# A layernorm, gated-MLP and attention kernel: front loads in one queue in order of need, and transposes placed a tile ahead of use

## The chip, the core and the metric

The kernel runs on one core of a Trainium2 chip. The metric is device time in microseconds (us); one execution is one number. "Before" and "changed" are the two kernels compared; the variants are named e1 to e13. Engines are named as in the profile: PE is TensorE's matmul, PEld its weight load, DVE is VectorE, ACT is ScalarE, POOL is GpSimd, SP is SyncE, which here only issues DMAs.

## The reference, cut to what matters

```python
def reference(A_x, A_k_cache, A_v_cache, A_wq, A_wo, B_x, B_W_gate, B_W_up, B_W_down):
    x = A_x                                    # 1 x 2048 x 512, bf16
    xn = _layernorm(x, axis=-1)
    s = _A_ref(xn, A_k_cache, A_v_cache, A_wq, A_wo)    # 32-head attention over cached K and V
    g = _silu(_B_ref(xn, B_W_gate, B_W_up, B_W_down))   # h = relu(xn Wg) * (xn Wu); h Wd; 512 -> 1792 -> 512
    return x + s * g
```

The gated MLP is computed first, from about 1 to 140 us, and attention fills the rest. The change touches only the first 20 us of code: the loads of `x` and of the gate and up weights, and the first quarter of the gate and up matmuls.

## The kernel before: the parts that matter

Rows of `x` are worked on in four row blocks of 512; a row block has four row tiles of 128. A weight has 14 column blocks (`FC`) of 128. For the first row block the kernel does not wait for the whole layernorm: it centres each row tile, transposes it on PE, and starts the first three column blocks tile by tile (128-column matmuls, "the head"). From column block 3 on it uses full-size matmuls of 512 columns.

The loads come from two queues, SP's and ACT's. Each weight is cut into three column pieces, at blocks 0, 3, 8 and 14:

```python
FCS = [0, min(3, FC), min(8, FC), FC]
HFC = 3
# load_w(engine, tile, source, semaphores, piece); load_x0(engine, row tile); load_xq(row block), on SP
load_x0(sp, 0)
load_x0(act, 1)
load_w(sp, Wg_sb, wg_src, sem_wg, 0)
load_w(act, Wu_sb, wu_src, sem_wu, 0)
load_x0(sp, 2)
load_x0(act, 3)
load_w(sp, Wg_sb, wg_src, sem_wg, 1)
load_w(sp, Wu_sb, wu_src, sem_wu, 1)
load_xq(1)
load_w(sp, Wg_sb, wg_src, sem_wg, 2)
load_w(sp, Wu_sb, wu_src, sem_wu, 2)
for Q in range(2, QB):
    load_xq(Q)
sem_wd.sig(sp.dma_start(Wd_sb[:], ...))
```

The head, with a warm-up of ten and two throw-away matmuls:

```python
warm_mm(10)                       # called just before head_ln
def head_ln():
    ctok = {0: head_transpose(0, head_center(0))}
    warm_mm(2)
    for n in range(4):
        if n + 1 < 4:
            ntok = head_center(n + 1)
        _wait(pe, ctok[n])
        head_tile(n, 0)
        if n + 1 < 4:
            ctok[n + 1] = head_transpose(n + 1, ntok)
        for fc in range(1, HFC):
            head_tile(n, fc)
```

The matmul results go to a ring of three slots, each with a gate bank and an up bank in PSUM. ACT applies the Relu, DVE multiplies, and the product frees the slot. In the same DVE stream, after the product of column block `fc`, come the layernorm statistics of row tile `4 + fc`, because those rows are needed next. DVE takes its instructions in the order of the program, so a product stands behind the statistics that were issued before it, and those wait for the rows to land.

```python
def finish_gate_up(Q, fc, s, gtok, gu_tok):
    # ... ACT: gr = relu(gate bank); DVE: hT = gr * up bank, signalled as h_tok
    ring_tok[s] = [rtok, h_tok]      # the next user of slot s waits for both
    if Q == 0:
        ln_task(fc)

def ln_task(i):
    if i < 4 * (QB - 1):
        ln_hold["st"] = ln_stats(4 + i)      # waits for load_xq((4 + i) // 4) where (4 + i) % 4 == 0
        # ... every fourth: aggregate, and Sqrt on ACT; from i = 4 on, coefficients and normalization on POOL
    # ...
```

The softmax here doesn't subtract the row's maximum and nothing guards it: scores larger than these inputs give would overflow.

Of the kernel before, what the change touches and what calls it, by code (L numbers as in the profile page):

```python
# [51 lines left out]
def bass_recurrent_scan__mha_block_cached__glu_gated_reglu__prompt_kernel(  # L52
# [18 lines left out]
    NQ = 512  # L71
# [33 lines left out]
    with ExitStack() as es:  # L105
# [27 lines left out]
        PT = [S_([128, 2, NQ], BF16, "PT") for _ in range(NPB)]  # L133
        warm = S_([128, D], BF16, "warm")
        es_b = ExitStack()
# [23 lines left out]
        sem_x0 = [newsem(16) for _ in range(4)]  # L159
        sem_wg = [newsem(16) for _ in range(3)]  # L160
        sem_wu = [newsem(16) for _ in range(3)]
        sem_xq = [newsem(16) for _ in range(QB)]
# [39 lines left out]
        with nc.Block() as block:  # L202

            @block.tensor
            def _(_pe_eng):
# [12 lines left out]

                FCS = [0, min(3, FC), min(8, FC), FC]
                HFC = 3  # L220
# [17 lines left out]

                warm_w = sem_ln1.sig(dve.memset(warm[:], 0.0))
                load_x0(sp, 0)  # L240
                load_x0(act, 1)
                load_w(sp, Wg_sb, wg_src, sem_wg, 0)
                load_w(act, Wu_sb, wu_src, sem_wu, 0)
                load_x0(sp, 2)
                load_x0(act, 3)
                load_w(sp, Wg_sb, wg_src, sem_wg, 1)
                load_w(sp, Wu_sb, wu_src, sem_wu, 1)
                if QB > 1:
                    load_xq(1)
                load_w(sp, Wg_sb, wg_src, sem_wg, 2)  # L250
                load_w(sp, Wu_sb, wu_src, sem_wu, 2)
                for Q in range(2, QB):
# [103 lines left out]
                def head_transpose(n, ntok):  # L356
# [13 lines left out]
                    return acc_free[n % 2]  # L370

                def warm_mm(k):
                    for _i in range(k):
                        pe.matmul(ps_r[:, 2 * NSLOT - 1, 0:D], warm[:, 0:128], warm[:], start=True, stop=True)  # L374

                def head_ln():
                    ctok = {0: head_transpose(0, head_center(0))}
                    warm_mm(2)
                    for n in range(4):
                        if n + 1 < 4:  # L380
                            ntok = head_center(n + 1)
                        _wait(pe, ctok[n])
                        head_tile(n, 0)
                        if n + 1 < 4:
                            ctok[n + 1] = head_transpose(n + 1, ntok)
                        for fc in range(1, HFC):
                            head_tile(n, fc)

                half_slots = []

                def head_tile(n, fc):
# [5 lines left out]
                    for i, (W, sems) in enumerate(((Wg_sb, sem_wg), (Wu_sb, sem_wu))):  # L397
                        if n == 0 and fc == 0:
                            pe.wait_ge(sems[0].h, 16)
                        ins = None  # L400
                        for c in range(DC):
                            ins = pe.matmul(ps_r[:, 2 * s + i, hs], W[:, c, fs], xcT[:, c, hs],  # L402
                                            start=(c == 0), stop=(c == DC - 1))
                        if n == 3:
                            half_tok[(fc, i)] = (sem_gate if i == 0 else sem_gu).sig(ins)
# [40 lines left out]
                hT_free = [None, None]  # L446

                def finish_gate_up(Q, fc, s, gtok, gu_tok):
                    par = Q % 2
                    gb = 2 * s  # L450
                    gk = fc % NSLOT
                    _wait(act, gtok)
                    _wait(act, gr_free[gk])
                    rtok = sem_relu.sig(act.activation(gr_sb[gk][:], ps_r[:, gb, :], ACTF.Relu))  # L454
                    _wait(dve, gu_tok)
                    _wait(dve, rtok)
                    if fc == 0:
                        _wait(dve, hT_free[par])
                    h_tok = sem_h.sig(
                        dve.tensor_tensor(hT[par][:, fc, :], gr_sb[gk][:], ps_r[:, gb + 1, :], ALU.mult)  # L460
                    )
                    gr_free[gk] = h_tok
                    ring_tok[s] = [rtok, h_tok]
                    if Q == 0:
                        ln_task(fc)
                    return h_tok

                def emit_gate_up(Q):
                    qs = slice(Q * NQ, (Q + 1) * NQ)
                    h_tok = None  # L470
                    for fc in range(FC):
                        fs = slice(fc * 128, (fc + 1) * 128)
                        if Q == 0 and fc < HFC:
                            s = half_slots[fc]
                            finish_gate_up(Q, fc, s, half_tok[(fc, 0)], half_tok[(fc, 1)])
                            continue
                        s = ring_acquire()
                        gb = 2 * s
                        if fc == 0:
# [7 lines left out]
                        for c in range(DC):  # L487
                            ins = pe.matmul(ps_r[:, gb, :], Wg_sb[:, c, fs], xT[:, c, xs],  # L488
                                            start=(c == 0), stop=(c == DC - 1))
                        gtok = sem_gate.sig(ins)  # L490
                        for c in range(DC):
                            ins = pe.matmul(ps_r[:, gb + 1, :], Wu_sb[:, c, fs], xT[:, c, xs],  # L492
                                            start=(c == 0), stop=(c == DC - 1))
# [44 lines left out]
                assert DC == 4 and QB >= 2 and FC >= 4 * (QB - 1) + 2  # L538
                _wait(pe, warm_w)
                warm_mm(10)  # L540
                head_ln()
# [354 lines left out]
```

## Time and profile before

| | |
|---|---|
| median of three runs | 1286.97 us (1286.95 to 1287.77) |
| span of the profiled execution | 1284.6 us (its time: 1286.42 us) |
| PE busy, of the span | 1278.8 us |
| chain of waits that ended last | 99% PE |
| first full-size gate matmul starts | 12.83 us |
| statistics of row tile 8 (row 1024) start | 19.46 us |

The first view is the busy time of each engine in chosen stretches. The columns are the stretch, its length, busy time and number of instructions of PE, PEld, DVE, ACT and POOL, granted clock, DMA share and GB/s.

```profile
1.19:6.21 5.02, 4.78 (x16) 1.76 (x16) 2.37 (x6) 2.07 (x3) 0.50 (x4) 1.00 0.87 273
6.21:12.83 6.62, 6.20 (x108) 6.06 (x109) 3.15 (x8) 3.25 (x6) 0.00 (x0) 1.00 1.07 363
12.83:140.00 127.17, 127.17 (x590) 57.62 (x591) 56.47 (x104) 40.40 (x71) 12.29 (x16) 1.00 0.32 70
140.00:1275.00 1135.00, 1135.00 (x11300) 767.25 (x11299) 310.85 (x551) 955.31 (x1029) 0.00 (x0) 1.00 0.28 51
```

PE is busy 127.17 of 127.17 us, then 1135.00 of 1135.00. After 12.83 us it has no idle time for an earlier load to remove. A change of the front can only win what lies before 12.83.

The second view is the timeline of before: start, duration, engine, line, operation, `output<-inputs`, shapes, count, and in brackets the idle time before the row and what ended it. It is shown up to the start of the first full-size group.

```profile
1.19 4.12 PE L374 MATMUL ps_r<-warm 128*128 128x512 bf16 x10 [1.19 <-DVE warm L239]
...
6.21 0.40 PE L402 MATMUL ps_r<-xcT,Wg_sb 128*128 128x128 bf16 x4 [0.25 <-ACT xcT L369]
...
12.03 0.39 PE L402 MATMUL ps_r<-xcT,Wu_sb 128*128 128x128 bf16 x4
12.83 1.02 PE L488 MATMUL ps_r<-xcT,Wg_sb 128*128 128x512 bf16 x4 [0.42 <-ACT gr_sb L454]
```

```profile
18.23 0.69 DVE L460 TENSOR_TENSOR hT<-gr_sb,ps_r 128x512 bf16<-128x512 bf16 x1 [0.92 <-PE ps_r L492]
19.46 0.69 DVE L319 BATCH_NORM_STATS2 stats<-x_sb 128x6 f32<-128x512 bf16 x1 [0.54 <-DMA x_sb<-in_A_x_dram]
...
20.35 0.69 DVE L460 TENSOR_TENSOR hT<-gr_sb,ps_r 128x512 bf16<-128x512 bf16 x1
```

```profile
20.60 1.03 PE L492 MATMUL ps_r<-xcT,Wu_sb 128*128 128x512 bf16 x4
21.46 1.03 PE L488 MATMUL ps_r<-xcT,Wg_sb 128*128 128x512 bf16 x4
22.33 1.03 PE L492 MATMUL ps_r<-xcT,Wu_sb 128*128 128x512 bf16 x4
```

PE lost 0.58 us before 12.83: the group of four before it started at 12.03, and four 128-column matmuls take 0.2226 us, so the next could have come at 12.25. At 19.46 DVE had waited 0.54 us for rows 1024 and up. The product behind these statistics ended at 20.35 + 0.69 = 21.04, and the matmuls that need its ring slot started at 21.46. So the load of these rows cost PE nothing, **with 0.42 us to spare**.

### The profile page before, as it was taken

To read this page: it belongs to the slowest core of one execution; us is meant where nothing else is said; L and a number is where in the kernel's file an instruction comes from. 1 tells how busy PE (TensorE), PEld (TensorE's weight loads), DVE (VectorE), ACT (ScalarE), POOL (GpSimd) and SP (SyncE) were. 2 spreads that over 40 slices of the span, in tenths; PEclk is the share of its full clock that TensorE was granted. 3 is DMA by queue.
4 is the path that set the end of the run, shared out by engine and by line. 5 is a ranking of instruction groups with operands and counts; after the bars stand their busy time and mean duration, and the time that the engine had idled before them with its cause. 6 is when DMAs were issued, how large, how long until landed. Compare 5 with 4: busy or idle time off the path is not lost.

```text
span 1284.6 us, 26946 instructions
## 1 busy us (share of the span) xinstructions
PE 1278.8 (100%) x12040; PEld 835.2 (65%) x12040; DVE 380.6 (30%) x685; ACT 1001.7 (78%) x1109; POOL 13.2 (1%) x25
## 2 busy tenths in 40 slices
PE   9999999999999999999999999999999999999998
PEld 5444476666666666666666666666666666666665
DVE  6433311112222222222222222222222222234455
ACT  3322399998888888888888888888888888888884
POOL 2100000000000000000000000000000000000000
PEclk9999999999999999999999999999999999999999
DMA  9600123232222332332321322323323312333202
GB/s 262 131 1 1 22 48 53 62 55 38 36 53 46 71 55 50 55 70 51 54 47 31 66 47 53 55 67 55 55 51 71 54 34 38 51 67 55 51 13 75
DMA packets 240977, 72.13 MB, mean 56 GB/s; under 512 B 227808, under 2 KB 240864, under 8 KB 240864
## 3 DMA queue, kind: packets, MB, share of 16 engines
q1 hardware_dynamic: 240048, 69.76, 28.5%
q8 instruction: 96, 1.57, 0.5%
q10 hardware_dynamic: 816, 0.66, 0.2%
q14 instruction: 17, 0.14, 0.0%
HBM read 32.77 MB, written 2.10 MB: 27 GB/s over the span
## 4 chain that ended last, share of the span: by engine, by line
PE 99%; DVE 1%; ACT 0%; issue 0%; DVEq 0%
PE ps_acc L742 36%; PE ps_r L645 34%; PE ps_r L578 9%; PE ps_r L599 8%; PE ps_acc L511 4%; PE ps_r L488 4%; PE ps_r L492 4%; PE ps_r L779 1%; DVE fin_tmp L787 0%; PE ps_r L402 0%; PE ps_r L374 0%; DVE x_sb L803 0%; ACT gr_sb L454 0%; PE ps_acc L364 0%; ACT xcT L369 0%
## 5 line engine op out<-in xcount | busy, mean ns | idle before, releaser
L655 ACT ACTIVATE PT<-ps_r 128x1024 bf16<-128x1024 f32 x1024 | 952.5, 1054 | 167.7 <-PE ps_r L645 167.7
L742 PEld LDWEIGHTS ps_acc<-V_sb,PT 128*128 128x128 bf16 x8192 | 620.9, 98 | 241.8 <-ACT PT L655 3.5
L742 PE MATMUL ps_acc<-V_sb,PT 128*128 128x129 bf16 x8192 | 776.9, 220 | 0.0
L645 PE MATMUL ps_r<-QT_sb,KT_sb 128*128 128x512 bf16 x2048 | 754.5, 379 | 0.0
L672 DVE RECIPROCAL rz_sb<-ps_acc 128x4 f32<-128x4 f32 x127 | 23.2, 183 | 729.8 <-PE ps_acc L742 729.8
L645 PEld LDWEIGHTS ps_r<-QT_sb,KT_sb 128*128 128x128 bf16 x2048 | 194.9, 98 | 1.1 <-DVE QT_sb L589 0.4
L578 PE MATMUL ps_r<-xnT,Wq_sb 128*128 128x512 bf16 x512 | 130.9, 379 | 0.0
L599 PE MATMUL ps_r<-Wo_sb,OT_store 128*128 128x512 bf16 x448 | 114.6, 379 | 0.0
L589 DVE CAST QT_sb<-ps_r 128x512 bf16<-128x512 f32 x128 | 88.5, 691 | 48.2 <-PE ps_r L578 48.2
L578 PEld LDWEIGHTS ps_r<-xnT,Wq_sb 128*128 128x128 bf16 x512 | 49.8, 97 | 60.7 <-ACT PT L655 27.1
L675 DVE TENSOR_TENSOR Onorm<-ps_acc,rz_sb 128x512 bf16<-128x512 f32 x127 | 87.8, 691 | 4.4
L599 PEld LDWEIGHTS ps_r<-Wo_sb,OT_store 128*128 128x128 bf16 x448 | 43.8, 98 | 52.9 <-ACT PT L655 0.2
L454 ACT ACTIVATE gr_sb<-ps_r 128x512 bf16<-128x512 f32 x56 | 32.9, 595 | 49.2 <-PE ps_r L488 48.7
L612 DVE TENSOR_TENSOR s_acc<-s_acc,ps_r 128x512 f32<-128x512 f32 x96 | 66.0, 687 | 17.4 <-PE ps_r L599 17.4
L460 DVE TENSOR_TENSOR hT<-gr_sb,ps_r 128x512 bf16<-128x512 bf16 x56 | 38.4, 685 | 46.9 <-PE ps_r L492 42.2
L511 PE MATMUL ps_acc<-Wd_sb,hT 128*128 128x512 bf16 x224 | 49.0, 379 | 0.0
L492 PE MATMUL ps_r<-xnT,Wu_sb 128*128 128x512 bf16 x168 | 43.1, 379 | 0.0
L488 PE MATMUL ps_r<-xnT,Wg_sb 128*128 128x512 bf16 x168 | 43.1, 379 | 0.0
L511 PEld LDWEIGHTS ps_acc<-Wd_sb,hT 128*128 128x128 bf16 x224 | 21.9, 98 | 26.5 <-DVE g_sb L528 0.3
L519 ACT ACTIVATE sig_sb<-ps_acc 128x512 f32<-128x512 f32 x12 | 7.2, 597 | 29.5 <-PE ps_acc L511 29.5
L492 PEld LDWEIGHTS ps_r<-xnT,Wu_sb 128*128 128x128 bf16 x168 | 16.4, 98 | 19.8
L488 PEld LDWEIGHTS ps_r<-xnT,Wg_sb 128*128 128x128 bf16 x168 | 16.4, 98 | 19.8
(50 smaller groups left out, 182.1 us busy)
## 6 DMA issues: line engine op xcount, KB each, us to landing
V_sb<-in_A_v_cache_dram SPq DMA_DIRECT2D x32, 512.0 KB, 4.6
Wq_sb<-in_A_wq_dram SPq DMA_DIRECT2D x32, 128.0 KB, 2.5
Wo_sb<-in_A_wo_dram SPq DMA_DIRECT2D x8, 512.0 KB, 4.9
OT_store<-Onorm SPq DMA_TRANSPOSE x127, 2.4
Wd_sb<-in_B_W_down_dram SPq DMA_DIRECT2D x1, 1792.0 KB, 14.6
x_sb<-in_A_x_dram SPq DMA_DIRECT2D x3, 512.0 KB, 12.1
out_dram<-x_sb SPq DMA_DIRECT2D x6, 256.0 KB, 2.2
Wg_sb<-in_B_W_gate_dram SPq DMA_DIRECT2D x1, 768.0 KB, 12.0
```

The lines of the kernel that those rows point to most:

```text
L460: dve.tensor_tensor(hT[par][:, fc, :], gr_sb[gk][:], ps_r[:, gb + 1, :], ALU.mult)
L488: ins = pe.matmul(ps_r[:, gb, :], Wg_sb[:, c, fs], xT[:, c, xs], start=(c == 0), stop=(c == DC - 1))
L492: ins = pe.matmul(ps_r[:, gb + 1, :], Wu_sb[:, c, fs], xT[:, c, xs], start=(c == 0), stop=(c == DC - 1))
L511: ins = pe.matmul(ps_acc[:, jb, 0:D], hT[par][:, fc, j * 128:(j + 1) * 128], Wd_sb[:, fc, :], start=(fc == 0), stop=(fc == FC - 1))
L578: ins = pe.matmul(ps_r[:, bank, :], Wq_sb[b][:, c, :], xnT[:, c, qs], start=(c == 0), stop=(c == DC - 1))
L589: etok = sem_qpe.sig(dve.tensor_copy(QT_sb[b][:, qs], ps_r[:, bank, :]))
L599: ins = pe.matmul(ps_r[:, bank, 0:D], OT_store[g % 2][:, hh, n * 128:(n + 1) * 128], Wo_sb[g % 2][:, hh, :], start=(hh == 0), stop=(hh == ...
L612: dve.tensor_tensor(s_acc[:, n, :], s_acc[:, n, :], ps_r[:, bank, 0:D], ALU.add)
L645: ins = pe.matmul(ps_r[:, 2 * s + tt, :], KT_sb[h % 2][:, t * 128:(t + 1) * 128], QT_sb[h % 2][:, qs], start=True, stop=True)
L655: act.activation(PT[pb][:], ps_r[:, 2 * s:2 * s + 2, :], ACTF.Exp, scale=scale)
L675: dve.tensor_tensor(Onorm[ob][:], o_ap, rz_sb[:].to_broadcast([128, 4, Dh]), ALU.mult))
L742: ins = pe.matmul(o_ap, PT[pb][:, tt, j * 128:(j + 1) * 128], V_sb[vb][:, t, 0:VW], start=(t == 0 and j % 2 == 0), stop=(t == KT - 1 and j ...
```

## The change

Its intent is fourfold: put all early loads but one into one queue, in the order in which they are needed, and cut the first need down to two column blocks of both weights; place each transpose a tile ahead of its use, so that PE does not wait for the copy out of PSUM; put column block 3 into the two accumulator banks, which are free by then, so that it needs no ring slot; and take the warm-up operand from a constant, which saves a memset, with fewer warm-up matmuls.

```diff
-                FCS = [0, min(3, FC), min(8, FC), FC]
+                FCS = [0, 2, 4, 6, 10, FC]
@@ loads (load_wgu(k) loads piece k of both weights, on SP)
-                warm_w = sem_ln1.sig(dve.memset(warm[:], 0.0))
                 load_x0(sp, 0)
                 load_x0(act, 1)
-                load_w(sp, Wg_sb, wg_src, sem_wg, 0)
-                load_w(act, Wu_sb, wu_src, sem_wu, 0)
+                load_wgu(0)
                 load_x0(sp, 2)
-                load_x0(act, 3)
-                load_w(sp, Wg_sb, wg_src, sem_wg, 1)
-                load_w(sp, Wu_sb, wu_src, sem_wu, 1)
-                if QB > 1:
-                    load_xq(1)
-                load_w(sp, Wg_sb, wg_src, sem_wg, 2)
-                load_w(sp, Wu_sb, wu_src, sem_wu, 2)
+                load_x0(sp, 3)
+                load_wgu(1)
+                load_wgu(2)
+                load_xq(1)
+                load_wgu(3)
+                load_wgu(4)
                 for Q in range(2, QB):
                     load_xq(Q)
@@ head
+                    c0 = head_transpose(0, head_center(0))
+                    warm_mm(1)
+                    c1 = head_transpose(1, head_center(1))
+                    n2 = head_center(2)
+                    n3 = head_center(3)
+                    _wait(pe, c0)
+                    head_tile(0, 0)
+                    head_tile(0, 1)
+                    _wait(pe, c1)
+                    head_tile(1, 0)
+                    head_tile(1, 1)
+                    c2 = head_transpose(2, n2)
+                    head_tile(0, 2)
+                    head_tile(1, 2)
+                    c3 = head_transpose(3, n3)
... (tiles 2 and 3 follow; the old loop is gone)
@@ gate and up
-                        s = ring_acquire()
-                        gb = 2 * s
+                        if Q == 0 and fc == HFC:
+                            s = None                    # the two accumulator banks
+                            _wait_all(pe, acc_free)
+                        else:
+                            s = ring_acquire()
+                        g_ps, u_ps = gu_banks(s)
@@ warm-up
-                warm_mm(10)
+                warm_mm(8)
... (weight waits per piece, five semaphores per weight, constants of 1.0 as warm-up operands)
```

More of the change, by code (lines that the diff above doesn't have):

```diff
@@ L133, in bass_recurrent_scan__mha_block_cached__glu_gated_reglu__prompt_kernel @@
         PT = [S_([128, 2, NQ], BF16, "PT") for _ in range(NPB)]
-        warm = S_([128, D], BF16, "warm")
         es_b = ExitStack()
@@ L159, in bass_recurrent_scan__mha_block_cached__glu_gated_reglu__prompt_kernel @@
         sem_x0 = [newsem(16) for _ in range(4)]
-        sem_wg = [newsem(16) for _ in range(3)]
-        sem_wu = [newsem(16) for _ in range(3)]
+        sem_wg = [newsem(16) for _ in range(5)]
+        sem_wu = [newsem(16) for _ in range(5)]
         sem_xq = [newsem(16) for _ in range(QB)]
@@ L237, in load_xq, with load_wgu @@
                         sp.dma_start(x_sb[:, 4 * Q:4 * Q + 4, :], x_t[:, 4 * Q:4 * Q + 4, :]))
-                warm_w = sem_ln1.sig(dve.memset(warm[:], 0.0))
+                def load_wgu(k):
+                    load_w(sp, Wg_sb, wg_src, sem_wg, k)
+                    load_w(sp, Wu_sb, wu_src, sem_wu, k)
                 load_x0(sp, 0)
                 load_x0(act, 1)
-                load_w(sp, Wg_sb, wg_src, sem_wg, 0)
-                load_w(act, Wu_sb, wu_src, sem_wu, 0)
+                load_wgu(0)
                 load_x0(sp, 2)
-                load_x0(act, 3)
-                load_w(sp, Wg_sb, wg_src, sem_wg, 1)
-                load_w(sp, Wu_sb, wu_src, sem_wu, 1)
-                if QB > 1:
-                    load_xq(1)
-                load_w(sp, Wg_sb, wg_src, sem_wg, 2)
-                load_w(sp, Wu_sb, wu_src, sem_wu, 2)
+                load_x0(sp, 3)
[4 more added lines that the diff above has]
+                load_wgu(4)
                 for Q in range(2, QB):
@@ L370, in head_transpose @@
                     return acc_free[n % 2]
+                ones_w = nc.const_aps.tensor(1.0, [128, 128], BF16)
+                ones_r = nc.const_aps.tensor(1.0, [128, NQ], BF16)
                 def warm_mm(k):
                     for _i in range(k):
-                        pe.matmul(ps_r[:, 2 * NSLOT - 1, 0:D], warm[:, 0:128], warm[:], start=True, stop=True)
+                        pe.matmul(ps_r[:, 2 * NSLOT - 1, :], ones_w, ones_r, start=True, stop=True)
                 def head_ln():
-                    ctok = {0: head_transpose(0, head_center(0))}
-                    warm_mm(2)
-                    for n in range(4):
-                        if n + 1 < 4:
-                            ntok = head_center(n + 1)
-                        _wait(pe, ctok[n])
-                        head_tile(n, 0)
-                        if n + 1 < 4:
-                            ctok[n + 1] = head_transpose(n + 1, ntok)
-                        for fc in range(1, HFC):
-                            head_tile(n, fc)
+                    c0 = head_transpose(0, head_center(0))
[13 more added lines that the diff above has]
+                    c3 = head_transpose(3, n3)
+                    _wait(pe, c2)
+                    for fc in range(HFC):
+                        head_tile(2, fc)
+                    _wait(pe, c3)
+                    for fc in range(HFC):
+                        head_tile(3, fc)
                 half_slots = []
@@ L397, in head_tile @@
                     for i, (W, sems) in enumerate(((Wg_sb, sem_wg), (Wu_sb, sem_wu))):
-                        if n == 0 and fc == 0:
-                            pe.wait_ge(sems[0].h, 16)
+                        if n == 0 and fc in FCS:
+                            pe.wait_ge(sems[FCS.index(fc)].h, 16)
                         ins = None
@@ L446, in _, with gu_banks @@
                 hT_free = [None, None]
+                def gu_banks(s):
+                    if s is None:
+                        return ps_acc[:, 0, :], ps_acc[:, 1, :]
+                    return ps_r[:, 2 * s, :], ps_r[:, 2 * s + 1, :]
                 def finish_gate_up(Q, fc, s, gtok, gu_tok):
                     par = Q % 2
-                    gb = 2 * s
+                    g_ps, u_ps = gu_banks(s)
                     gk = fc % NSLOT
@@ L453, in finish_gate_up @@
                     _wait(act, gr_free[gk])
-                    rtok = sem_relu.sig(act.activation(gr_sb[gk][:], ps_r[:, gb, :], ACTF.Relu))
+                    rtok = sem_relu.sig(act.activation(gr_sb[gk][:], g_ps, ACTF.Relu))
                     _wait(dve, gu_tok)
@@ L459, in finish_gate_up @@
                     h_tok = sem_h.sig(
-                        dve.tensor_tensor(hT[par][:, fc, :], gr_sb[gk][:], ps_r[:, gb + 1, :], ALU.mult)
+                        dve.tensor_tensor(hT[par][:, fc, :], gr_sb[gk][:], u_ps, ALU.mult)
                     )
                     gr_free[gk] = h_tok
-                    ring_tok[s] = [rtok, h_tok]
+                    if s is None:
+                        y_bank_free[:] = [h_tok, h_tok]
+                    else:
+                        ring_tok[s] = [rtok, h_tok]
                     if Q == 0:
@@ L476, in emit_gate_up @@
                             continue
-                        s = ring_acquire()
-                        gb = 2 * s
+                        if Q == 0 and fc == HFC:
+                            s = None
+                            _wait_all(pe, acc_free)
+                        else:
+                            s = ring_acquire()
+                        g_ps, u_ps = gu_banks(s)
                         if fc == 0:
@@ L487, in emit_gate_up @@
                         for c in range(DC):
-                            ins = pe.matmul(ps_r[:, gb, :], Wg_sb[:, c, fs], xT[:, c, xs],
+                            ins = pe.matmul(g_ps, Wg_sb[:, c, fs], xT[:, c, xs],
                                             start=(c == 0), stop=(c == DC - 1))
@@ L491, in emit_gate_up @@
                         for c in range(DC):
-                            ins = pe.matmul(ps_r[:, gb + 1, :], Wu_sb[:, c, fs], xT[:, c, xs],
+                            ins = pe.matmul(u_ps, Wu_sb[:, c, fs], xT[:, c, xs],
                                             start=(c == 0), stop=(c == DC - 1))
@@ L538, in _ @@
                 assert DC == 4 and QB >= 2 and FC >= 4 * (QB - 1) + 2
-                _wait(pe, warm_w)
-                warm_mm(10)
+                warm_mm(8)
                 head_ln()
```

## The prediction

> **What bounds the kernel now.** TensorE. The page gives PE 1278.8 us busy of a 1284.6 us span; the chain of waits is 99% PE. By stretches, PE is busy 127.17 of 127.17 us from 12.83 to 140 us, and 1135.00 of 1135.00 from 140 to 1275. So all that the change can win lies before the first full-size gate matmul, at 12.83 us; the rest only moves earlier by what the head saves.
>
> **The head of before (timeline).**
> - PE starts at 1.19, after the DVE memset of `warm`; ten warm-up matmuls, 0.43 us apart, fill it to 5.31.
> - Statistics of the first rows start at 3.47 (DVE waited 2.34 us for the load); centred at 4.77, copied by ACT at 6.15; first head matmul at 6.21.
> - 96 head matmuls and 12 transposes at 0.0557 us each (0.2226 us per four) end near 12.25.
> - Before 12.83 PE waits about 0.4 us. The view of waits names the ACT Relu, but the DVE product that frees the first ring slot ends at 12.73: that is the later one.
>
> **What the change does.**
> 1. Block 3 goes to the accumulator banks, which are free, not to ring slot 0. Block 4 asks for slot 0 about 1.7 us later, after its product. The wait at 12.4 to 12.8 goes: -0.4 to -0.5 us, on the critical path.
> 2. Tile 1's transpose stands before tile 0's matmuls. Its input, ready at 5.98, lets PE begin the dense run near 6.07. From there 108 x 0.0557 = 6.0 us: the head ends near 12.1, not 12.25: -0.15 to -0.2 us. Later transposes have 1 us or more of other work to hide their copies (0.58 us).
> 3. Loads: the first need is now 256 + 512 KB in place of 256 + 768, and tiles 2 and 3 come right after. Before moved 273 GB/s from 1.19 to 6.21. So weights should land near 4.7 to 5.3 (estimate), tile 2 before 5.98: DVE's 0.63 us wait for it vanishes. DVE needs 1.2 us per tile (0.69 + 0.18 + 0.35), ahead of PE. Off the chain; perhaps -0.05 us if the first tile lands sooner. More issues (0.45 us each on SP) and 512-byte runs use slack only.
> 4. Warm-up: no memset, PE starts near 0.8, but eight matmuls end near 4.2, and the first transpose waits till 4.9. Risk: the Trainium skill, "TensorE: Matmul & The Clock Gate", section on the HAM clock gate, says that full clock needs about 3.4 us of sustained activity in a free-running window. The trace agrees roughly: 0.43 us spacing through 4.6, 0.22 us per 512 columns from about 5.3, some 4 us after the start. With a hole, full clock may come up to 3.4 us later: at most 1.5 us lost, perhaps one execution in five. Estimated mean cost 0.2 us.
>
> **Sum.** -0.45 - 0.2 - 0.05 + 0.2 = -0.5 us: 1286.5 us, range 1285.6 to 1287.5. This is 0.04%, less than the spread of the three times before (0.8 us). Faster by over 2%: 0.003; within 2%: 0.994; slower by over 2%: 0.003.
>
> **What would show it.** First full gate matmul near 12.1 with no wait before it; head matmuls in one unbroken run from 6.1; no DVE wait for x tiles 2 and 3; busy PE from there to the end; the span shorter by the same shift.
>
> **What would make it wrong.** Cold matmuls (0.1 us at 128 columns) after 5 us; weights landing late because of short runs; DVE blocked in order by a late x load (rows 512 on) so that a ring slot is held; or the shift lost at a later fixed wait.

## More of the kernel before

A chip job runs several kernels on one chip, beside fresh runs of before.

The profiled execution was a little faster than the median, 1286.42 against 1286.97 us. That gap is as large as what we are looking for, so single profiles are read for where PE waits, and medians for the size. The timeline of before is shown in this section for two stretches around 20 us, one for DVE and one for PE.

## The result, and the profile after

| | before | changed |
|---|---|---|
| median (runs) | 1287.00 us (6) | 1287.67 us (6) |
| range | 1286.95 to 1287.77 | 1287.27 to 1288.27 |
| span of the profiled execution | 1284.6 us | 1285.5 us |
| first full-size gate matmul | 12.83 us | 12.54 us |
| statistics of row tile 8 | 19.46 us | 20.37 us |
| first Q-projection matmul (end of the MLP) | 140.60 us | 141.47 us |

The ratio was 1.0005, 95% interval 0.9992 to 1.0018. The medians say 0.67 us slower, where 0.5 us faster was predicted. No interval excludes 1. The argument therefore rests on waits seen in traces, and times support it.

The same stretches in the changed kernel, as busy time per engine:

```profile
12.83:140.00 127.17, 126.35 (x586) 56.93 (x585) 56.47 (x105) 40.48 (x70) 12.34 (x16) 1.00 0.33 74
140.00:1275.00 1135.00, 1135.00 (x11300) 767.39 (x11299) 310.72 (x550) 955.35 (x1029) 0.00 (x0) 1.00 0.28 51
```

After 140 us nothing differs: PE is busy without a gap again, and from the first Q-projection matmul to the end both spans take the same 1144.0 us (1284.6 - 140.60 and 1285.5 - 141.47). Between 12.83 and 140 us PE now has 127.17 - 126.35 = 0.82 us of idle time that before had not. The timeline shows where. First the head on PE:

```profile
0.78 3.21 PE L377 MATMUL ps_r<-const-bfloat16-1.0 128*128 128x512 bf16 x8 [0.78 <-PEq L905]
...
5.84 0.40 PE L364 MATMUL ps_acc<-ident,xc_sb 128*128 128x128 bf16 x4 [0.52 <-DVE xc_sb L354]
6.08 0.39 PE L415 MATMUL ps_r<-xcT,Wg_sb 128*128 128x128 bf16 x4
6.51 0.40 PE L415 MATMUL ps_r<-xcT,Wu_sb 128*128 128x128 bf16 x4
...
7.86 0.39 PE L415 MATMUL ps_r<-xcT,Wu_sb 128*128 128x128 bf16 x4
8.29 0.38 PE L364 MATMUL ps_acc<-ident,xc_sb 128*128 128x128 bf16 x4
8.51 0.39 PE L415 MATMUL ps_r<-xcT,Wg_sb 128*128 128x128 bf16 x4
8.96 0.40 PE L415 MATMUL ps_r<-xcT,Wu_sb 128*128 128x128 bf16 x4
...
12.32 0.39 PE L415 MATMUL ps_r<-xcT,Wu_sb 128*128 128x128 bf16 x4
12.54 1.03 PE L513 MATMUL ps_acc<-xcT,Wg_sb 128*128 128x512 bf16 x4
```

Then the stretch around 20 us, DVE and PE:

```profile
18.53 0.69 DVE L478 TENSOR_TENSOR hT<-gr_sb,ps_r 128x512 bf16<-128x512 bf16 x1 [0.92 <-ACT gr_sb L472]
20.37 0.69 DVE L319 BATCH_NORM_STATS2 stats<-x_sb 128x6 f32<-128x512 bf16 x1 [1.15 <-DMA x_sb<-in_A_x_dram]
...
21.25 0.69 DVE L478 TENSOR_TENSOR hT<-gr_sb,ps_r 128x512 bf16<-128x512 bf16 x1
```

```profile
20.31 1.03 PE L517 MATMUL ps_r<-xcT,Wu_sb 128*128 128x512 bf16 x4
22.09 1.02 PE L513 MATMUL ps_r<-xcT,Wg_sb 128*128 128x512 bf16 x4 [0.75 <-DVE hT L478]
22.95 1.03 PE L517 MATMUL ps_r<-xcT,Wu_sb 128*128 128x512 bf16 x4
```

The sum of PE's losses and gains, against before:

- The first full-size matmul comes at 12.54, not 12.83: **-0.29 us**. The wait before it is gone (12.32 + 0.22 = 12.54), but three steps of the head start 0.21 to 0.22 us later than the four matmuls before them allow: at 6.51 and 8.96, where the up weights were late, and at 8.29, for the transpose of tile 2.
- The group at 22.09 should have followed that of 20.31 by 0.864 us (four times 512 columns at 0.216), at 21.18. It came **0.91 us** later. DVE had waited 1.15 us for rows 1024 and up, which came at 20.37; the product behind their statistics ended at 21.25 + 0.69 = 21.94; PE started 0.15 us after it.
- One more wait of **0.24 us** stands before the third tile of the down projection, at 38.73 us, for the DVE result `g_sb`.

-0.29 + 0.91 + 0.24 = +0.86 us, and the Q projection starts 0.87 us later. The account is closed; what remains is why these waits arose.

### The profile page after: what moved, and what is told of

It is laid out like the page before. It is cut to its first block, busy times and chain, and to the rows that moved or that the text cites. A ratio compares the mean times of both kernels' runs of the same rounds, so it can differ in the third digit from the quotient of the medians. Undisturbed runs are those within 1.5% of the kernel's fastest.

```text
span 1285.5 us, 26943 instructions
## 1 busy us (share of the span) xinstructions
PE 1278.5 (99%) x12037; PEld 834.8 (65%) x12037; DVE 380.7 (30%) x684; ACT 1001.5 (78%) x1109; POOL 13.3 (1%) x25
## 4 chain that ended last, share of the span: by engine, by line
PE 96%; DVE 2%; DMA 1%; SPq 1%; issue 0%; ACT 0%; DVEq 0%; ACTq 0%
PE ps_acc L766 36%; PE ps_r L669 34%; PE ps_r L602 9%; PE ps_r L623 8%; PE ps_acc L536 3%; PE ps_r L513 3%; PE ps_r L517 3%; DMA x_sb<-in_A_x_dram 1%; SPq L226 1%; PE ps_r L803 1%; DVE fin_tmp L811 0%; DVE stats L319 0%; DVE hT L478 0%; DVE x_sb L827 0%; SPq L232 0%
## 5 line engine op out<-in xcount | busy, mean ns | idle before, releaser
L536 PEld LDWEIGHTS ps_acc<-Wd_sb,hT 128*128 128x128 bf16 x224 | 21.9, 98 | 26.7 <-DVE g_sb L553 0.6
```

Of the source, the lines that this page charges most:

```text
L536: ins = pe.matmul(ps_acc[:, jb, 0:D], hT[par][:, fc, j * 128:(j + 1) * 128], Wd_sb[:, fc, :], start=(fc == 0), stop=(fc == FC - 1))
```

## The experiments

Two theories for the wait at 22 us. *Late rows*: the rows from 1024 on land late, DVE stands in order behind their statistics, and the ring slot is held. *Ring order*: column block 3 has no slot now, so later blocks meet other slots, and the wait comes from that. And if the rows are what is late, why: short runs in memory (a run is a stretch of consecutive bytes; it is as long as a row of the piece), one queue, or the number of DMAs? Before's medians in the jobs below were 1286.85 (e1 to e4), 1286.97 (e5 to e8), 1286.96 (e9 to e12) and 1286.75 us (e13). All thirteen gave results that agree with the reference.

### e1: rows 1024 to 1535 ahead of the last pieces

```diff
                 load_wgu(3)
+                load_xq(2)
                 load_wgu(4)
-                for Q in range(2, QB):
-                    load_xq(Q)
+                load_xq(3)
```

> The changed kernel with one load moved: rows 1024 to 1535 of x are issued before the last pair of weight pieces, not after. Theory (late rows): in the changed kernel DVE stands in order behind the statistics of row tile 8 until those rows land at 20.34 us, the product behind it ends at 21.94, and PE loses 0.91 us at 22.09. Here the rows should land near 17.5, that wait of PE goes, nothing else changes in the first 20 us, and the time falls by 0.8 to 1.0 us to about 1286.8. Rival (ring order): the 0.91 us is a result of block 3 having no ring slot, so that later blocks meet slots that are not free yet; then the wait stays near 22 us and the time stays near 1287.7.

Measured: 1286.52 us (1285.95 to 1287.47), ratio 0.9998 (0.9986 to 1.0011), against 1.0005 for the changed kernel. The rows landed at 16.76 us. PE of e1 in the same place:

```profile
20.13 1.03 PE L517 MATMUL ps_r<-xcT,Wu_sb 128*128 128x512 bf16 x4
20.99 1.03 PE L513 MATMUL ps_r<-xcT,Wg_sb 128*128 128x512 bf16 x4
21.85 1.03 PE L517 MATMUL ps_r<-xcT,Wu_sb 128*128 128x512 bf16 x4
```

The groups follow each other by 0.86 us: the wait is gone, with the slots used as in the changed kernel. The wait at 38.7 is gone too. *Ring order* falls; *late rows* stands. The Q projection started at 140.13 us, 0.47 before that of before and 1.34 before that of the changed kernel. Of these 1.34 us, 0.91 and 0.24 are the two waits. The other 0.19 arose in the head (first full-size matmul at 12.356, not 12.543), where the two have the same loads: in this execution the first up weights happened to land at 5.87, not 6.46.

### e2 and e10: the statistics one block later

e2 leaves the loads alone and lets DVE do `ln_task(fc - 1)` after product `fc`, with the last two tasks together at the end.

```diff
-                    if Q == 0:
-                        ln_task(fc)
+                    if Q == 0 and fc > 0:
+                        ln_task(fc - 1)
+                        if fc == FC - 1:
+                            ln_task(fc)
```

> The changed kernel with the same loads in the same order; only the statistics of each row tile come one block later in DVE's order. Theory (late rows): the rows still land near 20.3 us, but the product that frees the ring slot no longer stands behind them, so the wait of 0.91 us at 22.09 goes or falls under 0.2, and the time falls by 0.7 to 1.0 us to about 1286.8. Rival (ring order): the wait stays, time near 1287.7. If the load itself were what PE needs (not DVE's order), the wait would stay as well.

Measured: 1287.48 us (1287.26 to 1288.28), no gain. The rows landed at 19.98. The wait at 22 us is gone as expected, but a new one came in its place, as the view of PE's waits shows (us in total, times, longest):

```profile
PE ps_acc L538 <- DVE g_sb L555: 0.8, 1, 0.8
```

The timeline puts it at 38.69 us, 0.95 us after the matmul before it could have been followed. The first sigmoid needs coefficients that come from the last statistics. e10 puts the statistics off only for row tiles 8 to 12 and catches up at block 9:

```diff
-                    if Q == 0:
-                        ln_task(fc)
+                    if Q == 0 and fc != 4:
+                        ln_task(fc if fc < 4 or fc > 9 else fc - 1)
+                        if fc == 9:
+                            ln_task(9)
```

> A mended form of the run in which the statistics came a block later: they are put off by one block only from row tile 8 to 12 and then catch up, so that the last ones come no later than in the changed kernel. There the wait at 22 us was gone but a wait of 0.95 us came at 38.7, because the coefficients for the first sigmoid came late. Theory (late rows, DVE in order): here both are small (under 0.3 each), with the rows still landing near 20 us, and the time is 0.6 to 0.9 below the changed kernel's: 1286.5 to 1287.1. Rival: a wait of 0.6 or more stays at either place.

Measured: 1287.15 us (1286.33 to 1287.69). The wait at 22 was gone again, but 0.71 us was lost at 38.67, so the expectation missed. In this profile an up-weight piece was late as well and cost 0.69 us at 9.34. Both runs show that DVE's order, not the load as such, holds the ring slot at 22 us. They also show that the order of DVE is no cure: the rows came at 20.89 in e10, and the chain from there (eight statistics between products, aggregate, Sqrt, coefficients, first sigmoid) ended at 38.61, as late as in the changed kernel (38.67). **The late rows are a limit in two places; e1, which brings them earlier, removes both.**

### e3: the order of work alone, with the loads of before

Edit: in the changed kernel, the load block and `FCS` of before.

> The changed kernel's order of work (transposes ahead, block 3 in the accumulator banks, warm-up from a constant) with the loads of before: same pieces, same two queues. Theory (the order of work gains, the loads give it back): Wu piece 0 near 6.2 us, first full-size gate matmul at 12.0 to 12.3 us (12.83 before, 12.54 changed), rows 1024 on at 19.4, a wait of PE of 0 to 0.4 us near 21 us, time 1286.4 to 1286.8. Rival (the order of work costs by itself): no faster than before, 1287.0 or more.

Measured: 1286.07 us, five times 1285.89, 1285.90, 1286.07, 1286.74 and 1287.83. The median is what the theory expected; the spread is not. The profiled execution was the slowest of the five, and it shows another thing altogether. Stretches of e3, with the granted clock third from the end:

```profile
3.94:7.35 3.41, 1.80 (x20) 1.09 (x20) 2.23 (x7) 1.17 (x2) 0.00 (x0) 1.00 1.08 361
7.35:10.76 3.41, 3.41 (x36) 3.41 (x34) 2.22 (x6) 0.37 (x1) 0.00 (x0) 0.50 1.08 362
10.76:14.24 3.48, 3.48 (x65) 3.48 (x63) 0.21 (x1) 1.72 (x4) 0.00 (x0) 1.00 1.07 369
```

```profile
7.03 0.39 PE L417 MATMUL ps_r<-xcT,Wu_sb 128*128 128x128 bf16 x4
...
8.44 0.63 PE L417 MATMUL ps_r<-xcT,Wu_sb 128*128 128x128 bf16 x4
...
11.12 0.39 PE L417 MATMUL ps_r<-xcT,Wu_sb 128*128 128x128 bf16 x4
```

The granted clock was 1.00, then 0.50 for 3.41 us, then 1.00 again. In the half-clock stretch four 128-column matmuls took 0.43 us from start to start, not 0.22. In 3.41 us PE did 36 instructions, where the next 3.48 us held 65. The first full-size gate matmul came at 14.24. This is the risk of the prediction's step 4. Its price, estimated as half of 3.41, is 1.7 us; the time of this execution lay 1.76 us over the median of the five. The prediction quoted the Trainium skill, "TensorE: Matmul & The Clock Gate", Part 1 on the HAM clock gate, for a free-running window of about 3.4 us; the 3.41 us here agree.

### e7, e9 and e11: the warm-up

e7 is e3 with the warm-up of before's length; e9 is the changed kernel with the same edit; e11 is e3 without any warm-up matmul.

```diff
-                warm_mm(8)
+                warm_mm(10)
@@ between the first two transposes
-                    warm_mm(1)
+                    warm_mm(2)
```

> The order of work alone (third run, e3) with the warm-up of before's length: 10 and 2 matmuls in place of 8 and 1. In e3's profile the granted clock fell back to half from 7.35 to 10.77 us, and its five times spread from 1285.89 to 1287.83. Theory (hole): the short warm-up leaves PE idle too long before the dense run, and some executions pay with a window of 3.4 us at half clock, 1.7 us of time. Then here no execution is over 1286.7, median 1285.9 to 1286.3. Rival (chance unrelated to the hole): the spread stays at over 1.5 us with times near 1287.8 among five.

> The changed kernel with 10 and 2 warm-up matmuls in place of 8 and 1, nothing else. The changed kernel's six times lie at 1287.27 to 1287.51 (three) and 1287.84 to 1288.27 (three). Theory (hole): the upper ones are executions in which TensorE lost its full clock for a while after the hole in the warm-up; without the hole the five times lie within 0.5 us, 1287.0 to 1287.5, and the late-rows wait of about 0.9 us stays in the profile. Rival (spread has another cause): times above 1287.8 still occur.

> The order of work alone (e3's kernel) without any warm-up matmul: the price of half clock measured by itself. Theory (hole): the dense run starts near 5.9 at half clock and stays there until a whole window has been busy, so the head runs at 0.11 us per 128-column matmul for 1 to 6 us: time 1286.9 to 1288.9, spread over 1 us. Rival (clock of no account): 1286.0 as with the long warm-up.

Measured: e7 1286.01 us (1285.97 to 1286.45), ratio 0.9994 (0.9981 to 1.0006); e9 1287.08 (1286.71 to 1287.27); e11 1287.42 (1287.03 to 1287.98, four runs). In e9's profile the wait for the late rows was 0.44 us at 21.53, where about 0.9 was expected: the rows landed at 19.78, though its loads are those of the changed kernel. In e7 PE was busy through the stretch in which e3 had a hole, and the clock did not fall:

```profile
3.94:7.35 3.41, 3.41 (x28) 2.02 (x27) 2.65 (x8) 1.17 (x2) 0.00 (x0) 1.00 1.07 359
7.35:10.76 3.41, 3.41 (x65) 3.41 (x63) 1.50 (x5) 1.17 (x2) 0.00 (x0) 1.00 1.08 361
```

In the second stretch e7 did 65 instructions, against e3's 36. (The clock column also reads 1.00 ahead of a trace's first clock record, while the warm-up matmuls still go 0.43 us apart; it is good for falls after that, as in e3.) With the long warm-up neither five spread by more than 0.56 us, about as the hole theory expected, and no time stood far above the rest. e11's profiled execution got full clock only at 10.84 us, by the trace's clock records; its first full-size matmul came at 14.38, against 12.34 in e7, and its time was 1287.98 against e7's 1285.97. So half clock in the head was worth about 2 us between these two profiles. (Some matmul records are missing from a trace. In e7 the first record of that group is at 12.56; its start is read from the group before it, 12.12 + 0.22. The same holds for e8 below.) What stays open is how much of the changed kernel's own spread (1287.27 to 1288.27) is this. Its one profile kept full clock from 3.49 us on, and e9's lower median may also come from its earlier rows. Before, with its long warm-up, itself spread from 1286.13 to 1287.59 in e9's job, so lost clock is not the only source of spread.

### e12: the accumulator banks alone

Edit: the kernel before with only the "gate and up" part of the diff.

> The kernel before with one part of the change: block 3 of the first row block goes to the accumulator banks instead of ring slot 0. Prediction's step 1: the wait before 12.83 goes, 0.4 to 0.5 us (the trace: 0.58 lost there). The rows from 1024 on land at 19.4 as before; in before the product behind them ended at 21.04 and its slot was wanted at 21.48, a slack of 0.44. PE 0.58 us earlier uses that up, so a wait of 0.1 to 0.3 near 21 us is expected and a gain of 0.3 to 0.5: 1286.4 to 1286.7. If the whole 0.58 shows, the slack was larger than read; if nothing shows, step 1 was worth nothing.

Measured: 1286.38 us (1285.86 to 1286.73), ratio 0.9996 (0.9982 to 1.0009). The first full-size matmul started at 12.44 with no wait before it, and there was no wait near 21 us: in this profile the rows landed at 19.00, earlier than in before's, so the small wait that was expected did not come. Step 1 of the prediction is worth what it said, about 0.4 us in the trace. It is also most of what the order of work has to give: e7, which adds the new order of transposes and the constant warm-up operand, started at 12.34.

### e4: the loads alone

Edit: the kernel before with the changed load block, five pieces, and a wait for each piece.

> The kernel before with the changed loads alone: five pieces of each weight, one queue. Its order of work takes all three blocks for tile 0 first, and the third block's up weights landed at 8.91 us in the changed kernel, where this order wants them near 7.6. Theory (the loads cost): PE waits about 1.2 to 1.4 us there, first full-size gate matmul near 14.1, no wait near 22 us since PE is late, time about 1288.3 (1287.9 to 1288.6). Rival (loads neutral): 1287.0 to 1287.3.

Measured: 1288.00 us (1287.36 to 1288.38), ratio 1.0009 (0.9996 to 1.0021): 1.15 us over before's median. In its profile the first full-size matmul came 14.10 - 12.83 = 1.27 us later than in before, and the Q projection as well (141.87 against 140.60), so all of it arose in the head. The groups at 7.88 and 8.78 were 0.35 and 0.66 us late; the wait before the first full-size group is that of before:

```profile
7.31 0.39 PE L404 MATMUL ps_r<-xcT,Wu_sb 128*128 128x128 bf16 x4
7.88 0.40 PE L404 MATMUL ps_r<-xcT,Wg_sb 128*128 128x128 bf16 x4 [0.18 <-DMA Wg_sb<-in_B_W_gate_dram]
8.78 0.40 PE L404 MATMUL ps_r<-xcT,Wu_sb 128*128 128x128 bf16 x4 [0.50 <-DMA Wu_sb<-in_B_W_up_dram]
...
13.26 0.39 PE L404 MATMUL ps_r<-xcT,Wu_sb 128*128 128x128 bf16 x4
14.10 1.02 PE L490 MATMUL ps_r<-xcT,Wg_sb 128*128 128x512 bf16 x4 [0.46 <-DVE hT L462]
```

The old order of work takes all three column blocks for tile 0 first, and the third was no longer in the first piece. So the loads and the new order belong together in the change. But even with that order the loads cost more than they bring: e3 and e7, with the old loads, have the lower medians.

### e5, e6 and e13: why the rows were late

e5 keeps the changed pieces but issues x tile 3 and the first two up-weight pieces from ACT's queue. e6 keeps the one queue but cuts the weights as in before. e13 is e7 with each weight piece loaded by two DMAs, each for half of the contraction rows.

```diff
@@ e5
-                load_wgu(0)
+                load_two(0)            # Wg piece on SP, Wu piece on ACT
                 load_x0(sp, 2)
-                load_x0(sp, 3)
-                load_wgu(1)
+                load_x0(act, 3)
+                load_two(1)
@@ e6
-                FCS = [0, 2, 4, 6, 10, FC]
+                FCS = [0, min(3, FC), min(8, FC), FC]
... (load_wgu(0), x tiles 2 and 3, load_wgu(1), load_xq(1), load_wgu(2), load_xq(2), load_xq(3))
@@ e13
-                        sems[k].sig(eng.dma_start(dst[:, :, a:b_], src[:, :, a:b_]))
+                        for c0 in (0, 2):
+                            sems[k].sig(eng.dma_start(dst[:, c0:c0 + 2, a:b_], src[:, c0:c0 + 2, a:b_]))
```

> The changed kernel with the same pieces in the same order, but x tile 3 and the first two up-weight pieces issued from ACT's queue. In the changed kernel DMA moved only 150 to 280 GB/s between 3.75 and 6 us, and 290 to 350 from 6 to 12. Theory A (short runs): the 512-byte packets are what is slow (27 to 31 ns each, 260 to 281 GB/s over 16 engines, against 346 for 1280 bytes); then the dip shrinks little and rows 1024 on still land at 19.8 us or later. Theory B (one queue): the single queue starves the engines early; then the dip goes (over 300 GB/s from 3 to 6 us), the first up weights land before 5.5 in place of 6.46, x tile 2 before 6.0 in place of 6.82, rows 1024 on at 19.0 to 19.5, and the time falls by 0.5 to 1.2 us.

> The changed kernel, still one queue in the same order of need, but with the three pieces per weight of before (768, 1280 and 1536-byte runs in place of 512 and 1024). Theory A (short runs): over 340 GB/s from 3 us on, rows 1024 on land near 19.2, the wait at 22 us falls under 0.3. Theory B (one queue): the dip to under 280 GB/s between 3.75 and 6 us stays, the first up weights land after 6.5 us, rows land at 19.7 or later. Both have the first need raised to 768 KB, so PE may wait up to 0.8 us near 6 us; time 1286.6 to 1287.6.

> The fastest variant so far (e7: changed order of work, loads of before, long warm-up), with each weight piece loaded by two DMAs, one for each half of the contraction rows: twice as many weight DMAs (12; the changed kernel has 10), half the bytes in each, the same 768, 1280 and 1536-byte runs. Theory (short runs made the rows late): rows 1024 on land at 18.8 to 19.4 us as in e7 (19.03), packets of 1280 bytes keep their 58 ns, no wait of PE near 21 us, time within 0.4 us of e7's 1286.0. Rival (the number of DMAs did it): rows land at 19.8 or later, as in all five runs with the changed loads in order, and a wait of 0.3 us or more comes back near 21 us.

The medians: e5 1286.90 us (1286.72 to 1287.15), e6 1286.37 (1286.20 to 1287.82), e13 1286.96 (1286.08 to 1287.39, four runs). In e5 and e6 neither theory came out whole. In e5 the dip of the DMA rate between 4 and 6 us went, as theory B says, but the rows stayed late, as theory A says, and the first up weights landed at 6.20, where B had them before 5.5. In e6 the rows came early and the wait at 22 us went, as theory A says, but the rate was 306 and not over 340 GB/s. The profiles, with rates from the stretches' last column and the landing of rows 1024 to 1535:

| kernel | queues for the first weights | runs of weights, bytes | weight DMAs | GB/s 4 to 6 us | GB/s 6 to 9 us | rows land, us |
|---|---|---|---|---|---|---|
| before | two | 768, 1280, 1536 | 6 | 358 | 363 | 19.44 |
| e7 | two | 768, 1280, 1536 | 6 | 353 | 367 | 19.03 |
| e6 | one | 768, 1280, 1536 | 6 | 306 | 341 | 19.00 |
| e13 | two | 768, 1280, 1536 | 12 | 279 | 359 | 19.73 |
| e5 | two | 512, 1024 | 10 | 340 | 295 | 20.16 |
| changed | one | 512, 1024 | 10 | 217 | 315 | 20.34 |

The lines for the changed kernel, e5 and e6 from which three rows of this table are read (the same columns as before):

```profile
4.00:6.00 2.00, 0.76 (x8) 0.46 (x9) 1.67 (x5) 0.59 (x1) 0.00 (x0) 1.00 0.81 217
6.00:9.00 3.00, 2.85 (x45) 2.36 (x44) 2.02 (x5) 0.88 (x2) 0.00 (x0) 1.00 1.09 315
```

```profile
4.00:6.00 2.00, 1.57 (x9) 0.67 (x9) 1.74 (x6) 0.84 (x3) 0.00 (x0) 1.00 1.12 340
6.00:9.00 3.00, 3.00 (x50) 2.92 (x49) 2.25 (x6) 0.98 (x2) 0.00 (x0) 1.00 1.20 295
```

```profile
4.00:6.00 2.00, 0.94 (x6) 0.29 (x5) 1.86 (x6) 0.59 (x1) 0.00 (x0) 1.00 1.06 306
6.00:9.00 3.00, 2.86 (x47) 2.63 (x48) 1.97 (x6) 0.75 (x2) 0.00 (x0) 1.00 1.01 341
```

Single profiles differ: with the changed kernel's front loads as they are (changed, e1, e2, e4, e9, e10) the rate between 4 and 6 us was 217 to 270 GB/s. So the table is read for large differences only.

- *One queue* is not what made the rows late. e5 lifts the rate to 340 GB/s between 4 and 6 us, but the rows land at 20.16, among those of the one-queue profiles (19.78 to 20.89), and 0.98 us is lost at 21.9 us. e6 keeps the one queue, and the rows land at 19.00. The head of e5 shows almost no wait (0.07 us), but that is partly luck: its clock record turns to full only at 6.61, so its dense run began at half clock, some 0.4 us behind (steps of 0.40 and 0.43 where full clock takes 0.22), and late weights were less late for it. In e8, at full clock from 4.54 us and with the same first pieces on two queues, the up weights come late again. The start of e5's dense run:

```profile
5.79 0.60 PE L368 MATMUL ps_acc<-ident,xc_sb 128*128 128x128 bf16 x4
6.19 0.59 PE L419 MATMUL ps_r<-xcT,Wg_sb 128*128 128x128 bf16 x4
6.62 0.39 PE L419 MATMUL ps_r<-xcT,Wu_sb 128*128 128x128 bf16 x4
```

- *Short runs* slow DMA after 6 us: 295 and 315 GB/s against 341 to 367. In the trace's DMA records between 6 and 12 us, a 512-byte packet took 29.2 ns on average in the changed kernel and 33.0 in e5, a 1280-byte packet 59.1 in before. Sixteen engines with one packet after another would move 281 and 248 against 346 GB/s. Packets overlap a little (a DMA share of 1.09 and 1.20 from 6 to 9 us above), so what was delivered is the 315 and 295 of the table.
- *The number of DMAs* seems to count as well, by one profile, which I had not expected: in e13, with long runs, the dip between 4 and 6 us came back (279 GB/s), the second half of the first up weights landed at 7.88, PE lost 0.47 us at 6.77 and 0.94 at 7.93, and the rows landed at 19.73. The expectation for e13 failed: neither side had it right. After 6 us its rate was that of before.

All six profiles with 10 weight DMAs and short runs and with the rows last (changed, e2, e4, e5, e9, e10) had the rows at 19.78 to 20.89; all six with 6 DMAs and long runs (before, e3, e6, e7, e11, e12) at 18.83 to 19.44. e6 differs from the changed kernel in the cut of the weights and almost nothing else (the rows from 512 on stay behind the pieces that the head needs), and its rows come 1.34 us sooner. So the fine cut of the weights is what made the rows late; how much of it is run length and how much the number of DMAs is not settled, as the runs with short pieces have both.

### e8: the combination

e8 has the changed order of work, two queues for the first pieces, pieces at blocks 0, 2, 4, 8 and 14, rows from 512 on before the third and rows from 1024 on before the last pair of pieces, and the long warm-up.

> What the theories together recommend: the changed order of work, two queues for the first pieces, pieces of 2, 2, 4 and 6 blocks, rows 512 on before the third and rows 1024 on before the last pair of pieces, warm-up of 10 and 2 matmuls. Theory: weights and x tiles land by 6 us, no wait of PE between 6.1 and the end over 0.2 us, first full-size gate matmul at 11.9 to 12.1, no wait near 22; time 1285.8 to 1286.2, 0.8 to 1.0 below before. If waits of 0.3 or more remain in the head, one of the loads was mis-sized.

Measured: 1286.21 us (1285.59 to 1286.32), ratio 0.9994 (0.9981 to 1.0006). The rows land at 15.71 and nothing waits near 22 us, but the up weights come late again in the head: 0.11, 0.26 and 0.22 us were lost at 6.39, 8.44 and 8.89. The first full-size matmul came at 12.47 us, where 11.9 to 12.1 was expected. It is no better than e7. Of all variants e7 has the lowest median, 0.96 us under before; its five times (1285.97 to 1286.45) all lie under the nine of before in its job (1286.57 to 1287.15). It is the change without its loads and without its shorter warm-up.

## Why the prediction was wrong

The measured 1287.67 us lies 0.17 above the range of 1285.6 to 1287.5; the sign was wrong. "Within 2%" was right, but either sign lay within it.

- *What bounds the kernel*: right. PE, and what the head loses or wins arrives unchanged at the end (1144.0 us from the Q projection on, in both).
- *Step 1, the accumulator banks, -0.4 to -0.5*: right. The wait before the first full-size matmul is gone; e12 alone moves that matmul by 12.83 - 12.44 = 0.39 us, and its median is 0.58 below before's.
- *Step 2, transposes ahead, head ends near 12.1*: the mechanism was right, the size was off. The dense run began even sooner than expected (5.84, not 6.07), but three waits of 0.21 to 0.22 us came into it and it ended at 12.54. The loads made all three: two are for up weights, and the transpose of tile 2 waited for rows that DVE got at 6.84. With the old loads, in e7, the dense run began at 6.27, behind the longer warm-up, had no wait and ended at 12.34.
- *Step 3, the loads*: **this step failed**, in the sentences "weights should land near 4.7 to 5.3", "tile 2 before 5.98" and "More issues and 512-byte runs use slack only". The first up weights landed at 6.46 in the changed kernel, tile 2 at 6.82 (in the six profiles with these front loads at 5.84 to 6.59 and 6.21 to 6.95). DVE's wait for tile 2 did not vanish but grew from 0.63 to 1.06 us. The slack of the rows from 1024 on was 0.42 us. The fine cut moved them 0.9 us later and the faster head wanted them 0.29 sooner: 0.9 + 0.29 - 0.42 = 0.77 us (an estimate), and 0.91 was lost. The rest is the 0.15 us from the end of the product to the matmul at 22.09, which the 0.42 leaves out: the slack that could be used was nearer 0.27. The prediction named this very failure ("DVE blocked in order by a late x load (rows 512 on) so that a ring slot is held") but gave it no number. The number could be read from before: DVE's wait for these rows, the end of the product behind it, and the start of the matmuls that use its slot.
- *Step 4, the clock, +0.2*: not seen in the changed kernel's profile, where full clock came at 3.49 us, sooner than before (4.85). That was luck: in the seven profiles with the short warm-up (changed, e1, e2, e3, e5, e6, e10) the first record of full clock lies anywhere from 3.49 to 6.61. The risk was real: e3 shows it in one execution, at an estimated 1.7 us. Its share in the changed kernel's times stays open.

In the sum, -0.45 - 0.2 was roughly sound for steps 1 and 2 without the new loads (e7: 0.96 below before in medians, but 0.45 in the profiles, by the start of the Q projection at 140.15; what makes the other half of the 0.96 is open). The term for the loads, entered as -0.05, was in truth 0.64 us in the three waits of the head, plus 0.91 + 0.24 after it. In the head 0.23 of it was hidden, as the dense run began that much sooner than predicted.

## What to carry to other kernels

Before you refine the front of a kernel, follow every load, not only the first: for each one behind the pieces you re-cut, read its landing, what it holds up in the order of its engine, and how much slack its last user has. A faster start eats that slack from one side and a slower queue from the other, so a gain of 0.3 us can turn into a loss of 0.9 at a place 10 us later. When loads in order of need must be cut finely, keep the later pieces long (e6 against the changed kernel; a fine first piece with long ones behind it, as in e8, was no faster than e7), and don't let a hole stand in the warm-up just before the dense run.

## What the Trainium skill lacked or had wrong

- "DMA: Bandwidth & Descriptors", section Specifications, gives 512 B as the least transfer for line rate. Here, between 6 and 12 us, 512-byte packets took 29.2 (changed) to 33.0 ns (e5) on average, which is 281 and 248 GB/s over 16 engines if none overlap, against 346 for 1280-byte packets (59.1 ns). Delivered between 6 and 9 us were 315 and 295 GB/s, against 341 to 367 with pieces of long runs: taken alone the figure misleads, as 512 bytes was not yet full rate.
- The same page, section "Issuing engines are not separate DMA queues", says that a second issuing engine only saves the sequencer's issue time, usually small beside the DMA. With the same pieces, the rate between 4 and 6 us was 217 to 270 GB/s with one queue (six profiles) and 340 with two (e5), so at a kernel's start the second queue was worth something; whether that is issue time isn't shown. It agrees that it brought little in the end: the rows landed at 20.16, where one queue gave 19.78 to 20.89 us.
- The same page, beyond its rule to batch DMAs to at least 1 MiB, has no cost for many DMAs of medium size in flight from SP and ACT: twice as many weight DMAs of half the size, at the same run length, moved 279 GB/s between 4 and 6 us where 353 had been (e13 and e7, one profile each), and the rows landed 0.70 us later.
- "TensorE: Matmul & The Clock Gate", Part 1, says that the clock falls back after at least one idle window of about 3.4 us. The length agrees (3.41 us at half clock in e3), but the window before it was not idle: PE was busy 1.80 of 3.41 us. The page gives no threshold for a partly busy window. In these traces full clock outlasted a window with 2.04 us busy (e13, 4.90 to 8.31) and one with 2.11 (changed, 3.49 to 6.90), so by these runs the limit lies between 1.80 and 2.04 of 3.41 us, if PE's busy time alone decides.
